# Low halves of the first layer's weight tiles: written by VectorE instead of GpSimd

## The chip, the cores and the metric

The kernel runs on one core of one Trainium2 chip. The metric is device time in microseconds (us) from launch to end. Before the change three runs gave a median of 1679.97 us (1676.94 to 1680.24).

## What is computed

```python
def _attn_ref(q, k, v):                       # 8 batches, 8 heads, 576 rows, 64 columns
    q_s = softmax(q, axis=-1); k_s = softmax(k, axis=2)
    kv = np.einsum('bhsd,bhse->bhde', k_s, v)
    return np.einsum('bhsd,bhde->bhse', q_s, kv)

def reference(q, k, v, moe_w_in, moe_w_out, moe2_w_in, moe2_w_out):
    x = attn.transpose(0, 2, 1, 3).reshape(4608, 512)
    h = x @ moe_w_in;  x = (h * sigmoid(1.702 * h)) @ moe_w_out       # 512 -> 2048 -> 512
    h = x @ moe2_w_in; return np.maximum(0.01 * h, h) @ moe2_w_out
```

All is float32. The two softmaxes are written out in the reference with max, exp and sum.

## The kernel before

**Split numbers.** A matrix product is made of three passes: each float32 operand is split into a high half (rounded by a ScalarE cast, line 80, `split_hi`) and a low half (the operand less the high half, line 83, `split_lo`). TensorE then adds high x high, low x high and high x low. Every weight tile and every activation tile therefore needs a cast on ScalarE and one subtraction before TensorE can finish its product. In the trace all subtractions have line 83 and are told apart by their tile.

**Chunks and layers.** The 4608 tokens are nine chunks of 512. In a layer, after some start, chunks go in pairs. The first product of a pair is a 2x2 block scheme that saves multiplications: `quad_step` (eight per pair, n = 0 to 7) takes a quarter of `w_in` (four tiles wa, wb, wc, wd, line 621), with sums and differences of token blocks (x and xb from xr) as the other operand. The second product (`g2`, line 668) goes over 16 slices f of `w_out` (tile wo) and accumulates in four PSUM banks (acc). `pair_first` runs the eight quad steps of a pair with the second product of its first chunk two slices behind; `pair_second` then runs the second product of the other chunk, f = 0 to 15.

**Where the low halves in question are made.** Chunk 1 of layer 0 goes through `pair_second` with `made` true: for f = 2 to 15 the float32 slice of `w_out` is loaded from DRAM (o, line 276, two buffers, and line 857 to 860: the load of slice f + 3 stands ahead of the making of slice f + 2), cast by ScalarE (`make_wo`), subtracted (`make_wo_low`, line 283) and stored to DRAM for the later pairs (line 284). The store and the load share SyncE's queue, which is in order. The quad tiles for chunk pair (2, 3) of layer 0 are made too: `s0` loads a quarter of `w_in` (w, line 215), `s1` makes two sums and differences from it (t, lines 222 to 224), and `make_tile` with `make_low` (line 241) split the four tiles and store them (line 242): wa (m = 0) and wd (m = 3) are plain quarters of w, wb and wc come from t. That is eight quads; quad 0 is made during `pair_second` of chunk 1, quad n + 1 during quad step n. All later pairs of the layer load split tiles from DRAM. In layer 1 the same is made again from its own weights.

**What stands around it.** In the same stretch the attention of chunks 2 and 3 runs in pieces between the products: row maxima of k (kmx, kma, km, kmb, lines 379 to 406), k less its maximum (line 412), exp, the product with v (kvp, line 427), its scale (krs and kv, lines 439 to 444), q (qmx, qt, qsm, qs, lines 450 to 469), its transpose (qtp, line 481), and the product that gives the tokens (pxt, line 503). After the start these use a single PSUM bank, `att` in `bank`, for kma, kmb, qtp and kvp. Then `build_pair` makes the token blocks (lines 549 and 566) and splits them (x, xb). Activations g of the second product have their own low halves (gl).

**What sets the order.** Each engine works through its own queue in order. The program is written with gaps into which work is put, and a scheduler of the framework then orders the instructions of all engines by its own estimate of when each is ready. Changing the engine of an instruction therefore also moves others.

Of the kernel before, what the change touches and what calls it, by code (L numbers as in the profile page):

```python
# [8 lines left out]
F32 = mybir.dt.float32  # L9
F32R = mybir.dt.float32r  # L10
AF = mybir.ActivationFunctionType
ALU = mybir.AluOpType
# [14 lines left out]
def tile_softmax_linear_attention_two_mlps(  # L27
# [16 lines left out]
    nc = tc.nc  # L44
# [34 lines left out]
    def split_hi(src, hi):  # L79
        nc.scalar.copy(hi, src)  # L80

    def split_lo(src, hi, lo, engine=nc.vector):
        engine.tensor_tensor(out=lo, in0=src, in1=hi.bitcast(F32), op=ALU.subtract)  # L83

# [41 lines left out]
    WO = {}  # L128
# [38 lines left out]
    def c4(f):  # L167
        w = cvt.pop(f)[:, 1, :].bitcast(F32)
        split_lo(w[:, 0:T].rearrange("p (b n) -> p b n", b=2), WI[f][:, :, 0, :], WI[f][:, :, 1, :])
        split_lo(w[:, T : 2 * T], WO[f][:, 0, :], WO[f][:, 1, :])  # L170
        n, i = divmod(f, 2)
        for b in range(2):
            nc.sync.dma_start(out=w4d[0][n][:, BLOCK[i, b], :], in_=w[:, 2 * P * b : 2 * P * (b + 1)])
        if f < 2:
            nc.sync.dma_start(out=wod[0][f], in_=WO[f].rearrange("p h n -> p (h n)").bitcast(F32))
        else:
            nc.sync.dma_start(out=o32d[0][f], in_=w[:, T : 2 * T])
# [60 lines left out]

    def make_low(i, n, m):
        src, to = halves.pop(m)  # L240
        split_lo(src, to[:, :, 0, :], to[:, :, 1, :], nc.gpsimd if i == 0 and m in (0, 3) else nc.vector)
        nc.sync.dma_start(
            out=wqd[i][n][:, 2 * m * T : (2 * m + 2) * T], in_=to.rearrange("p b h n -> p (b h n)").bitcast(F32)
        )
# [23 lines left out]
    o32 = {}  # L268
# [11 lines left out]
        split_hi(o32[f], WO[f][:, 0, :])  # L280

    def make_wo_low(i, f):
        split_lo(o32.pop(f), WO[f][:, 0, :], WO[f][:, 1, :], nc.vector if i else nc.gpsimd)
        nc.sync.dma_start(out=wod[i][f], in_=WO[f].rearrange("p h n -> p (h n)").bitcast(F32))


# [563 lines left out]
    def pair_second(layer, c, per_step):  # L850

        acc = new_acc()

        made = (layer, c) == (0, 1)
        ready(1)
        if made:
            load_o32(0, 2)
        for f in range(NF):
            if made and f + 3 < NF:
                load_o32(0, f + 3)  # L860
            if f + 2 < NF:
                if made:
                    make_wo(f + 2)
                    make_wo_low(0, f + 2)
                else:
                    load_wo(layer, f + 2)
                ready(f + 2)
            run(per_step.get(f, ()))
            if f < NF - LAG:
                g2(layer, f, acc, range(KT))  # L870
        return (layer, c, acc)
# [148 lines left out]
    def first_quad(layer, c):  # L1020

        if not sums_of(layer, c):
            return [lambda m=m: load_quad(layer, 0, m) for m in (0, 1, 2, 3)]
        made = (0, 3, 1, 2)
        pieces = [lambda: s0(layer, 0), lambda: s1(layer, 0)]
        for m in made:
            pieces += [lambda m=m: make_tile(layer, 0, m), lambda m=m: make_low(layer, 0, m)]
        pieces += [lambda: s0(layer, 1), lambda: s1(layer, 1)]
        return pieces

    def work_of(layer, c, nxt):
        def work(n, gaps):
            m = n + 1
            if m < NQ:
                if sums_of(layer, c):
                    def make(at, j):
                        gaps[at].append(lambda: make_tile(layer, m, j))
                        gaps[at + 1].append(lambda: make_low(layer, m, j))

                    make(1, 0)  # L1040
                    make(4, 3)
                    if m + 1 < NQ:
                        gaps[5].append(lambda: s0(layer, m + 1))
                    make(6, 1)
                    make(8, 2)
                    if m + 1 < NQ:
                        gaps[9].append(lambda: s1(layer, m + 1))
                else:
                    gaps[1].append(lambda: load_quad(layer, m, 1))
                    gaps[4].append(lambda: load_quad(layer, m, 0))  # L1050
                    gaps[5].append(lambda: load_quad(layer, m, 2))
                    gaps[9].append(lambda: load_quad(layer, m, 3))
            if (layer, c) == (1, 0):
                gaps[3].append(lambda: make_wo(2 * n))
                gaps[4].append(lambda: make_wo_low(1, 2 * n))
                gaps[7].append(lambda: make_wo(2 * n + 1))
                gaps[8].append(lambda: make_wo_low(1, 2 * n + 1))
                if n + 1 < NQ:
                    gaps[9].append(lambda: load_o32(1, 2 * n + 2))
                    gaps[9].append(lambda: load_o32(1, 2 * n + 3))  # L1060
            else:
                gaps[2].append(lambda: load_wo(layer, 2 * n))
                gaps[7].append(lambda: load_wo(layer, 2 * n + 1))
# [123 lines left out]
```

## Time and profile before

| | |
|---|---|
| median of three runs | 1679.97 us (1676.94 to 1680.24) |
| the profiled execution: its own time, its span | 1681.45 us, 1679.7 us |
| TensorE matmul (PE) busy | 1624.8 us, 97% of the span, 7552 instructions |
| VectorE (DVE) busy | 1050.3 us, 63%, 1649 instructions |
| ScalarE (ACT) busy | 640.5 us, 38%, 1088 instructions |
| GpSimd (POOL) busy | 120.8 us, 7%, 236 instructions |
| mean granted TensorE clock | 0.992 of full speed |

The profile was taken on one execution; its span runs from the first to the last instruction. PE is matmul, PEld weight load. An idle time in brackets behind an instruction names what its engine waited for. Full granted clock (1.00) is 2.4 GHz, half is 1.2 GHz.

### The profile page before, as it was taken

What the parts mean: (1) busy time and instruction counts of PE and PEld (TensorE: products, weight loads), DVE (VectorE), ACT (ScalarE), POOL (GpSimd) and SP (SyncE); (2) the same over time, 40 slices, a digit from 0 to 9 for tenths busy, and PEclk for the clock granted to TensorE, in tenths of its full rate; (3) what the DMA queues carried; (4) which work ended last, traced back from release to release, by engine and by line L of the source; (5) the groups of instructions that cost most, each with busy time, mean ns of one, the idle gap of its engine ahead of it and who ended that gap; (6) DMA issues with size and microseconds to landing.
All of it is one profiled execution on the core that took longest, in us unless ns stands there. A gap on an engine that the chain in (4) does not pass through costs nothing.

```text
span 1679.7 us, 21410 instructions
## 1 busy us (share of the span) xinstructions
PE 1624.8 (97%) x7552; PEld 1300.8 (77%) x7552; DVE 1050.3 (63%) x1649; ACT 640.5 (38%) x1088; POOL 120.8 (7%) x236
## 2 busy tenths in 40 slices
PE   5799998999999999999999999999999999999999
PEld 3577776777777778777888888888888888888887
DVE  8999657887767767667434877355734473445222
ACT  5667554555444445345223434211321132112222
POOL 1110243231100000000000000000000000000000
PEclk9999998999999999999999999999999999999999
DMA  7666476878888887878786876766676666667662
GB/s 216 216 217 204 124 236 238 291 259 265 271 272 253 248 265 238 287 255 305 261 270 219 312 279 230 253 219 187 208 252 209 196 216 216 213 190 225 200 208 100
DMA packets 192875, 391.50 MB, mean 233 GB/s; under 512 B 57600, under 2 KB 99584, under 8 KB 192768
## 3 DMA queue, kind: packets, MB, share of 16 engines
q1 hardware_dynamic: 192768, 390.14, 71.2%
q8 instruction: 60, 0.98, 0.2%
q14 instruction: 47, 0.39, 0.1%
HBM read 304.61 MB, written 85.46 MB: 232 GB/s over the span
## 4 chain that ended last, share of the span: by engine, by line
PE 80%; DMA 6%; DVE 4%; issue 2%; ACT 2%; POOL 2%; SPq 1%; ACTq 0%; POOLq 0%; DVEq 0%
PE acc L668 40%; PE hb L621 11%; PE h L608 9%; PE ha L621 8%; PE hc L621 8%; DMA o<-cv 2%; DMA w<-cv 2%; PE pxt L503 1%; DMA w<-w 1%; PE kvp L427 1%; DVE cv L125 1%; POOL wo L83 1%; DVE cv L121 1%; DVE gl L83 1%; POOL qt L451 0%
## 5 line engine op out<-in xcount | busy, mean ns | idle before, releaser
L668 PE MATMUL acc<-gh,wo 128*128 128x512 f32 x1152 | 367.5, 401 | 9.2 <-ACT gh L80 4.2
L668 PE MATMUL acc<-wo,gh 128*128 128x512 f32 x1152 | 355.8, 390 | 0.0
L668 PEld LDWEIGHTS acc<-gh,wo 128*128 128x128 f32 x1152 | 214.6, 191 | 57.4 <-ACT gh L80 5.5
L668 PEld LDWEIGHTS acc<-wo,gh 128*128 128x128 f32 x1152 | 216.2, 188 | 46.7 <-issue 0.4
L668 PE MATMUL acc<-gl,wo 128*128 128x512 f32 x576 | 226.5, 396 | 0.0
L668 PE MATMUL acc<-wo,gl 128*128 128x512 f32 x576 | 225.2, 391 | 0.0
L608 PE MATMUL h<-x,wi 128*128 128x512 f32 x768 | 194.5, 402 | 5.3 <-ACT wi L80 5.3
L608 PEld LDWEIGHTS h<-x,wi 128*128 128x128 f32 x768 | 143.2, 189 | 44.1 <-ACT wi L80 7.7
L83 DVE TENSOR_TENSOR gl<-gb,gh 128x512 fp32r<-128x512 f32 x128 | 91.0, 715 | 121.7 <-ACT gh L80 121.5
L621 PE MATMUL ha<-x,wa 128*128 128x512 f32 x624 | 165.6, 400 | 0.0
L80 ACT CAST gh<-gf 128x512 fp32r<-128x512 f32 x160 | 99.0, 619 | 136.9 <-PE acc L668 63.9
L83 DVE TENSOR_TENSOR gl<-gf,gh 128x512 fp32r<-128x512 f32 x160 | 110.4, 690 | 58.8 <-ACT gh L80 57.5
L80 ACT CAST gh<-gb 128x512 fp32r<-128x512 f32 x128 | 79.2, 621 | 161.3 <-PE acc L668 160.7
L621 PEld LDWEIGHTS ha<-x,wa 128*128 128x128 f32 x624 | 116.5, 188 | 29.0 <-issue 1.9
L668 PEld LDWEIGHTS acc<-gl,wo 128*128 128x128 f32 x576 | 109.3, 190 | 24.9 <-DVE gl L83 0.4
L668 PEld LDWEIGHTS acc<-wo,gl 128*128 128x128 f32 x576 | 108.1, 188 | 23.6
L777 DVE TENSOR_TENSOR u<-hb,p 128x512 f32<-128x512 f32 x56 | 38.5, 688 | 118.8 <-PE hb L621 110.0
L621 PE MATMUL hb<-x,wc 128*128 128x512 f32 x384 | 100.3, 396 | 0.8 <-DVE v L777 0.8
L621 PE MATMUL hb<-xb,wb 128*128 128x512 f32 x336 | 87.9, 396 | 2.7 <-ACT xb L80 2.7
L621 PEld LDWEIGHTS hb<-x,wc 128*128 128x128 f32 x384 | 71.7, 187 | 18.8 <-DVE v L777 1.9
L621 PEld LDWEIGHTS hb<-xb,wb 128*128 128x128 f32 x336 | 63.3, 189 | 18.2 <-ACT xb L80 3.0
L621 PE MATMUL hc<-x,wb 128*128 128x512 f32 x288 | 76.0, 399 | 0.9 <-DVE p L777 0.9
(131 smaller groups left out, 2073.7 us busy)
## 6 DMA issues: line engine op xcount, KB each, us to landing
wo<-wo SPq DMA_DIRECT2D x274, 512.0 KB, 4.2
wa<-wq SPq DMA_DIRECT2D x40, 512.0 KB, 4.0
wb<-wq SPq DMA_DIRECT2D x40, 512.0 KB, 4.6
wc<-wq SPq DMA_DIRECT2D x40, 512.0 KB, 4.7
raw<-in_moe_w_in_dram SPq DMA_DIRECT2D x32, 512.0 KB, 4.3
raw<-in_moe_w_out_dram SPq DMA_DIRECT2D x32, 512.0 KB, 4.9
wi<-wq SPq DMA_DIRECT2D x32, 512.0 KB, 4.5
wd<-wq SPq DMA_DIRECT2D x40, 256.0 KB, 3.2
```

The costliest lines, as they stand in the source:

```text
L80: nc.scalar.copy(hi, src)
L83: engine.tensor_tensor(out=lo, in0=src, in1=hi.bitcast(F32), op=ALU.subtract)
L121: nc.vector.scalar_tensor_tensor(out=w[:, o], in0=hw, scalar=0xC0000000, in1=w[:, o], op0=ALU.bitwise_and, op1=ALU.bitwise_or)
L125: nc.vector.tensor_tensor(out=w, in0=w, in1=low, op=ALU.add)
L427: nc.tensor.matmul(pk[h * D : (h + 1) * D, 0 : D + 1], rest[0][:, h, :] if r == R and rest else km[:, h, r, :], vm[:, h, r, :] if r < R el ...
L503: nc.tensor.matmul(pv[:, :, a:e], kvb[b, j], t[:, :, a:e], start=True, stop=True)
L608: nc.tensor.matmul(h, WI[f][:, b, wh, o * P : (o + 1) * P], xs[f"a{side}{b + 1}"][xh][:, o, :], start=(i == 0), stop=(i == n - 1),)
L621: nc.tensor.matmul(h, w[:, wh, o * P : (o + 1) * P], xo[xh][:, o, :], start=(start and i == 0), stop=(i == 5), skip_group_check=not start,)
L668: nc.tensor.matmul(acc[d], lhsT, rhs, start=(f == 0 and i == 0), stop=(f == NF - 1 and i == 2))
L777: add = lambda out, h, t: nc.vector.tensor_tensor(out=out, in0=h, in1=t, op=ALU.add)
```

## The change

The optional engine of `split_lo` goes away, and the three places that called it take VectorE always. In layer 0 the low halves of wo for f = 2 to 15 (14 instructions) and of wa and wd in the eight quads (16 instructions) were on GpSimd; they are now on VectorE. Layer 1 had them on VectorE already. Nothing else is edited.

```diff
-    def split_lo(src, hi, lo, engine=nc.vector):
-        engine.tensor_tensor(out=lo, in0=src, in1=hi.bitcast(F32), op=ALU.subtract)
+    def split_lo(src, hi, lo):
+        nc.vector.tensor_tensor(out=lo, in0=src, in1=hi.bitcast(F32), op=ALU.subtract)
...
     def make_low(i, n, m):
         src, to = halves.pop(m)
-        split_lo(src, to[:, :, 0, :], to[:, :, 1, :], nc.gpsimd if i == 0 and m in (0, 3) else nc.vector)
+        split_lo(src, to[:, :, 0, :], to[:, :, 1, :])
...
     def make_wo_low(i, f):
-        split_lo(o32.pop(f), WO[f][:, 0, :], WO[f][:, 1, :], nc.vector if i else nc.gpsimd)
+        split_lo(o32.pop(f), WO[f][:, 0, :], WO[f][:, 1, :])
```

The scheduler's order moves with it. First place, VectorE's queue at the start of `pair_second` of chunk 1 (o_2267 and o_2269 are the float32 slices f = 2 and 3; w_2371 and t_2439 are quad 0's quarter and its sums):

```order
 L401 TENSOR_REDUCE km<-kma 128x1
-L83 TENSOR_TENSOR gl<-gb,gh 128x512
+L83 TENSOR_TENSOR wo<-o_2267,wo 128x512
+L83 TENSOR_TENSOR gl<-gb,gh 128x512
+L83 TENSOR_TENSOR wo<-o_2269,wo 128x512
 L222 TENSOR_TENSOR t_2439<-w_2371 128x2x256
+L83 TENSOR_TENSOR wa<-w_2371,wa 128x2x256
+L412 TENSOR_TENSOR kt<-kt,kmb 128x640
+L83 TENSOR_TENSOR gl<-gb,gh 128x512
 L223 TENSOR_TENSOR t_2439<-w_2371,t_2439 128x256
-L412 TENSOR_TENSOR kt<-kt,kmb 128x640
```

Between km and line 412 there were a gl and lines 222 and 223; now there are two low halves of wo, a gl, line 222 and a low half of wa.

Second place, VectorE's queue of the changed kernel near the end of the same `pair_second`, where the token blocks of chunks 2 and 3 are built (o_2603 and o_2627 are slices f = 12 and 13):

```order
L566 TENSOR_TENSOR xr<-xr 128x1024
L379 TENSOR_REDUCE kmx<-kt 128x128
L83 TENSOR_TENSOR gl<-gb,gh 128x512
L83 TENSOR_TENSOR x<-xr,x 128x1024 x2
L549 TENSOR_TENSOR xr<-xr 128x1024
L83 TENSOR_TENSOR wo<-o_2603,wo 128x512
L83 TENSOR_TENSOR gl<-gb,gh 128x512
L83 TENSOR_TENSOR xb<-xr,xb 128x1024
L83 TENSOR_TENSOR wo<-o_2627,wo 128x512
```

The low half of slice 12 now stands behind the sum of line 566, two low halves of x and a difference of line 549; before it was in GpSimd's queue, where nothing of these stood.

Third place, TensorE's queue where the first quad step meets the last slices (acc_2259 to acc_2262 are the four banks of the second product):

```order
 L621 MATMUL ha<-x,wa 128x512 x6
 L396 MATMUL kma<-ident,kmx 128x128
-L621 MATMUL hb<-xb,wb 128x512 x3
 L668 MATMUL acc_2259<-gh,wo 128x512
 L668 MATMUL acc_2260<-gh,wo 128x512
+L668 MATMUL acc_2261<-gh,wo 128x512
+L668 MATMUL acc_2262<-gh,wo 128x512
 L668 MATMUL acc_2259<-gh,wo 128x512
 L668 MATMUL acc_2259<-gl,wo 128x512
```

Half of the product hb, which needs xb, stood ahead of slice 12; now it comes behind slices 12 and 13.

## Rows read from the trace of the kernel before

**Rows 1.** Busy time of stretches (length, then PE, PEld, DVE, ACT, POOL, clock).

```profile
218.00:296.00 78.00, 68.60 (x308) 52.98 (x306) 55.37 (x70) 38.58 (x65) 32.65 (x30) 0.91 0.73 249
...
260.00:280.00 20.00, 15.78 (x51) 11.80 (x51) 12.19 (x15) 6.94 (x11) 8.04 (x5) 0.74 0.53 198
296.00:400.00 104.00, 103.73 (x562) 82.77 (x563) 86.14 (x146) 55.04 (x100) 28.27 (x47) 1.00 0.81 269
880.00:1030.00 150.00, 150.00 (x652) 122.05 (x651) 102.59 (x166) 58.62 (x97) 0.00 (x0) 1.00 0.76 265
```

**Rows 2.** TensorE's waits, 210 to 400 us: total us, times, longest us.

```profile
PE hb L621 <- ACT xb L80: 2.7, 1, 2.7
PE acc L668 <- POOL wo L83: 2.3, 2, 1.6
PE pxt L503 <- ACT kv L444: 2.1, 2, 1.8
PE qtp L481 <- DVE kt L412: 1.5, 1, 1.5
PE hb L621 <- DVE u L777: 1.1, 1, 1.1
```

**Rows 3.** GpSimd's groups by form (busy us, mean ns, idle before).

```profile
L83 POOL TENSOR_TENSOR wo<-o,wo 128x512 fp32r<-128x512 f32 x14 | 22.1, 1593 | 30.0 <-ACT wo L80 27.8 <-DMA kt<-in_k_dram 2.2
...
L83 POOL TENSOR_TENSOR wa<-w,wa 128x512 fp32r<-128x512 f32 x8 | 11.8, 1477 | 23.3 <-ACT wa L80 16.5 <-PE kvp L427 6.8
L83 POOL TENSOR_TENSOR wd<-w,wd 128x512 fp32r<-128x512 f32 x8 | 10.8, 1350 | 18.9 <-ACT wd L80 18.9
```

**Rows 4.** Line 83 by form: durations ns min, median, max; first and last start us.

```profile
L83 DVE TENSOR_TENSOR wo<-o,wo x16: 682/692/693, 914.6 to 1026.6; 128x512 fp32r<-128x512 f32 x16
```

**Rows 5.** VectorE's groups by form, 216 to 297 us.

```profile
L83 DVE TENSOR_TENSOR gl<-gb,gh 128x512 fp32r<-128x512 f32 x13 | 12.3, 950 | 2.8 <-ACT gh L80 2.7
...
L223 DVE TENSOR_TENSOR t<-w,t 128x256 f32<-128x256 f32 x3 | 3.7, 1234 | 0.1
...
L222 DVE TENSOR_TENSOR t<-w 128x512 f32<-128x512 f32 x3 | 3.2, 1054 | 0.7 <-DMA w<-w 0.7
```

**Rows 6.** VectorE's timeline, 219 to 232 us (start us, length us, instruction).

```profile
219.56 1.61 DVE L83 TENSOR_TENSOR gl<-gb,gh 128x512 fp32r<-128x512 f32 x1
221.09 1.78 DVE L222 TENSOR_TENSOR t<-w 128x512 f32<-128x512 f32 x1
222.91 1.38 DVE L223 TENSOR_TENSOR t<-w,t 128x256 f32<-128x256 f32 x1
224.22 0.81 DVE L412 TENSOR_TENSOR kt<-kt,kmb 128x640 f32<-128x640 f32 x1
...
231.62 0.14 DVE L439 TENSOR_SCALAR krs<-kvp 128x1 f32<-128x1 f32 x1
```

**Rows 7.** GpSimd's timeline, three of its low halves of wo.

```profile
219.33 3.00 POOL L83 TENSOR_TENSOR wo<-o,wo 128x512 fp32r<-128x512 f32 x2
...
252.36 3.50 POOL L83 TENSOR_TENSOR wo<-o,wo 128x512 fp32r<-128x512 f32 x2 [2.20 <-DMA kt<-in_k_dram]
264.47 4.70 POOL L83 TENSOR_TENSOR wo<-o,wo 128x512 fp32r<-128x512 f32 x2 [8.61 <-ACT wo L80]
```

**Rows 8.** SyncE's queue, 205 to 300 us: its longest wait.

```profile
SPq L284 <- POOL wo L83: 33.6, 9, 8.2
```

**Rows 9.** Loads of the float32 slices o.

```profile
DMA to landing us min/median/max: 3.2/3.9/5.0
```

**Rows 10.** VectorE's timeline in two of the later quad steps.

```profile
328.84 0.69 DVE L777 TENSOR_TENSOR u<-hb,p 128x512 f32<-128x512 f32 x1 [0.42 <-PE kma L396]
...
360.51 0.41 DVE L223 TENSOR_TENSOR t<-w,t 128x256 f32<-128x256 f32 x1
...
364.81 0.69 DVE L777 TENSOR_TENSOR u<-hb,p 128x512 f32<-128x512 f32 x1 [2.22 <-PE kma L396]
365.42 0.28 DVE L401 TENSOR_REDUCE km<-kma 128x1 f32<-128x128 f32 x1
```

## The prediction

> **What bounds the kernel now.** I read the summary of the page first: PE is busy for 97% of the span, so only stretches where it is not are worth anything. Then I asked where GpSimd makes low halves (its groups by form, [rows 3]): 14 of wo and 16 of wa and wd, 44.7 us together, all between 219 and 386 us. The busy time by stretches [rows 1] splits that in two. From 218 to 296 us, the second product of chunk 1 with the start of the first quad steps, PE is busy for 68.60 of 78.00 us and its clock is 0.91 of full. From 296 to 400 us, the later quad steps, PE is busy for 103.73 of 104.00 us at full clock. So the first stretch alone can gain, and the second can only lose.
>
> What the first stretch loses: 78.00 - 68.60 = 9.4 us of idle time [rows 1]. A mean clock of 0.91 over 78 us is (1 - 0.91) x 2 x 78 = 14.0 us at the half level, of which (1 - 0.74) x 2 x 20 = 10.4 lie between 260 and 280 us [rows 1]. About 1.6 us of this is idle already (the longest wait for a GpSimd wo [rows 2]), and the rest does in 12.4 us what 6.2 would do, so 6.2 us are lost. Together 15.6 us: that is all there is to win.
>
> TensorE's waits [rows 2] name the ends: 2.7 us for an xb cast, 2.3 for wo from GpSimd, 2.1 for kv from ScalarE, 1.5 for line 412 and 1.1 for u, both on VectorE. Only 2.3 us name GpSimd. The next question is what made VectorE late.
>
> **What GpSimd did to VectorE.** The timelines of both [rows 6, 7] lie side by side: while GpSimd runs two low halves of wo from 219.33 to 222.33, VectorE's gl takes 1.61 us and its line 222 takes 1.78; their undisturbed length is about 0.69 [rows 4, 10]. Line 223 takes 1.38 there and 0.41 where GpSimd is quiet [rows 6, 10]. Both sides suffer: a pair of GpSimd's takes 3.00, 3.50 or 4.70 us [rows 7]. Over 216 to 297 us the groups give the excess [rows 5]: gl 13 x (0.95 - 0.69) = 3.4 us, line 223 3 x (1.23 - 0.41) = 2.5, line 222 3 x (1.05 - 0.69) = 1.1, so 7.0 us from these three groups alone.
>
> **The change part by part.** Removed from GpSimd: 30 instructions, 44.7 us [rows 3]. It is busy for 7% of the span, so this is worth only what waited for it. Added to VectorE: 30 instructions of a kind that it does in 0.69 us [rows 4]; followed by another of its own, one costs 0.61 from start to start (364.81 to 365.42 [rows 10]). That is 18.3 us, of which 20 x 0.61 = 12.2 fall before 296 us (14 wo and three pairs wa, wd), against at least 7.0 given back there. VectorE is busy for 55.37 of 78 us [rows 1], so it would have 60.6 at most to do; in the 66 us that I expect of this stretch, that is dense but fits.
>
> The Trainium skill (Perfetto Trace Analysis, Optimizing Scalar/DVE Operations) advises that work may be offloaded from a saturated VectorE, even to GpSimd, and adds that it might not help, because the two share a read port. By the first half alone this change would cost up to those 18.3 us; by the second half much of it was being paid already, and the stretched rows side with the second half here.
>
> Now by places, in the order of time. At the head (first place of the change), line 412 stood behind a stretched gl and lines 222 and 223, and started at 224.22 [rows 6]. Now five instructions stand between 219.56 and it, 5 x 0.61 = 3.05, so it starts near 222.6, 1.6 us earlier: the wait of 1.5 us on it [rows 2] goes. Next is kv, whose scale krs started at 231.62 [rows 6]. In the new queue 11 instructions stand between line 412 and krs, nine full ones and lines 223 and 224: 222.6 + 0.8 + 9 x 0.61 + 2 x 0.41 = 229.7, 1.9 us earlier. TensorE comes 1.5 us earlier but has one matmul more to do ahead of pxt (0.23, the 150 us over 652 of [rows 1]), so of its longest wait for kv, 1.8 us, about 1.2 remain.
>
> The slices wo come by a loop: a low half frees a buffer, SyncE (in order) stores it and loads the slice after next, the load lands 3.9 us later [rows 9], ScalarE casts it, then comes the next low half. SyncE waited 33.6 us for GpSimd's wo here [rows 8]. Two low halves take 1.2 us instead of 3.0 to 4.7 [rows 7], so each turn of the loop, two slices, is some 2 to 3 us shorter, and the 2.3 us of waits for wo should go. TensorE wants 12 x 0.23 = 2.8 us for a slice.
>
> What is late next is slice 12 (second place). Its low half now stands behind line 566, a reduction, a gl, two low halves of x and line 549. Counted in instructions of 512 elements, that is 2 + 2 + 1 + 4 + 2 = 11, and its own, 12 x 0.61 = 7.3 us. The gl of slice 13 is among them, and those of slices 11 and 12 stand just ahead, so I take VectorE to reach line 566 when TensorE begins slice 11. TensorE has slice 11, the product ha and four passes for the high half of slice 12, (12 + 6 + 4) x 0.23 = 5.1 us. So it waits about 2.2 us there. The wait of 2.7 us for xb goes, as that product now comes behind slices 12 and 13 (third place) and xb is made while they run.
>
> The wait of 1.1 us for u comes from line 223 ahead of it on VectorE; u now stands ahead of lines 222 and 223, so it goes. In the first quad step w's second quarter is loaded behind one store fewer, so I cost this at nothing; if it landed late, line 222 would hold up the v behind it.
>
> The later quad steps: two low halves more for each, 1.2 us of a step of (364.81 - 328.84) / 2 = 18.0 us [rows 10]. VectorE is busy for 83% (86.14 of 104 [rows 1]), hence 14.9 us of a step, and 16.1 after. The new wa stands ahead of u, which waits 0.42 us for TensorE in one step and 2.22 in another [rows 10]; line 223, stretched by the same wa before, gives back what it takes. I cost it at nothing; without that cover it is 0.2 to 1.2 us a step.
>
> **The sum.** Lost before 15.6; after, 1.2 + 2.2 = 3.4 idle. I keep one half-level spell as before's shorter one, 14.0 - 10.4 = 3.6 us, which costs 1.8, since the trace has it behind waits of 1.5 and 1.8 and I leave one of 2.2. Gain 15.6 - 3.4 - 1.8 = 10.4 us. The profiled execution took 1681.45, so 1671.0; it lay 1.5 above the median of the runs, so I forecast 1670 us. Bounds from both sides: everything gone gives 1680 - 15.6 = 1664; nothing gone gives 1680.
>
> **The rivals.** First, the same direction but less: VectorE holds slices 12 to 15 up while it builds the blocks, TensorE waits as long as before there, and the long half-level spell of 10.4 us comes back. Then only the head (1.5 + 0.6 + 1.8 of clock) and u (1.1) are won, 5.0 us: 1675. For it: the pile of 7.3 us ahead of slice 12. Against it: it needs VectorE 2 us later than counted.
>
> Second, no change: the loads bind the loop, not the halves. A load is 3.2 to 5.0 us [rows 9], and with SyncE's other transfers between, TensorE could meet the same slices late by as much. Then the waits only change their names and 0 to 3 us are won: 1678. Against it: SyncE's longest wait is for GpSimd [rows 8].
>
> Third, slower: VectorE becomes the bound of the quad steps. In eight steps 2 x 0.61 each go straight onto TensorE's path, because u, v and p free the banks that the next products need: 9.8 us, and with nothing won at the head 1690. It decides once VectorE's 3 us of slack in a step are less than its waits for the others. For it: u has only 0.42 us to spare in one step. Against it: in layer 1 the same tiles are made wholly on VectorE from 880 to 1030 us, and PE is busy for 150.00 of 150 us [rows 1], though without attention work beside it.
>
> **How the numbers follow.** The forecast (gain 7 to 15.6) has 0.60, the first rival 0.17, the second 0.14, the third 0.09. Runs of this kernel can tell 0.2% (3.4 us) from no change: faster is 0.77, within it 0.14, slower 0.09. The range goes from 1664.5, all waits gone, up to 1678, which leaves the third rival and half of the second outside; the likeliest case's own range is 1664.5 to 1673.
>
> **What would show it.** In the changed profile: PE idle from 218 on down from 9.4 to some 3.5 us, with slice 12 the longest wait and no wait for line 412 or u; VectorE's gl and lines 222 and 223 near 0.69 and 0.41; the clock between 260 and 280 us near full; later quad steps still of 18.0 us. Wrong it would be if the quad steps grew longer, if the half level stayed for 10 us, or if the waits for wo were now for loads.

## The result, and the profile after

The changed kernel takes 1665.66 us (median of 4 runs, 1661.06 to 1666.67), the kernel before 1679.49 (4 runs beside it, 1676.94 to 1680.24). The ratio is 0.9915, 95% interval 0.9893 to 0.9937. That is faster by 13.8 us; 10 were forecast.

The busy time by stretches comes first (length, then PE, PEld, DVE, ACT, POOL, clock; changed kernel). It answers to [rows 1].

```profile
218.00:296.00 78.00, 76.45 (x386) 60.23 (x385) 68.59 (x111) 45.75 (x79) 3.83 (x15) 1.00 0.89 306
260.00:280.00 20.00, 19.90 (x85) 15.45 (x84) 19.74 (x30) 12.10 (x20) 2.12 (x2) 1.00 0.92 312
```

In the 78 us where everything was to be won, TensorE is now idle for 78.00 - 76.45 = 1.55 us instead of 9.4, and its clock is full instead of 0.91. It runs 386 matmuls there instead of 308. From 260 to 280 us VectorE is busy for 19.74 of 20 us: that stretch has hardly any slack on VectorE left, and TensorE is still busy for 19.90.

TensorE's waits from 210 to 400 us (total us, times, longest us) are only these two, where [rows 2] has five:

```profile
PE pxt L503 <- ACT kv L444: 1.2, 2, 1.0
PE acc L668 <- DVE wo L83: 0.4, 1, 0.4
```

VectorE's timeline in the changed kernel (start us, length us, instruction) answers to [rows 6] in its first five lines and to [rows 10] in its last two; the two between belong to slice 12. The stage began 0.93 us later here than before, for a reason ahead of it (the first matmul of acc in it starts at 215.70 and started at 214.77), so 0.93 is to be taken off when starts are compared.

```profile
220.77 0.68 DVE L83 TENSOR_TENSOR gl<-gb,gh 128x512 fp32r<-128x512 f32 x1
...
222.15 0.69 DVE L222 TENSOR_TENSOR t<-w 128x512 f32<-128x512 f32 x1
...
223.41 0.81 DVE L412 TENSOR_TENSOR kt<-kt,kmb 128x640 f32<-128x640 f32 x1
...
224.74 0.42 DVE L223 TENSOR_TENSOR t<-w,t 128x256 f32<-128x256 f32 x1
...
230.23 0.15 DVE L439 TENSOR_SCALAR krs<-kvp 128x1 f32<-128x1 f32 x1
...
251.07 1.22 DVE L566 TENSOR_TENSOR xr<-xr 128x1024 f32<-128x1024 f32 x1
...
257.55 0.69 DVE L83 TENSOR_TENSOR wo<-o,wo 128x512 fp32r<-128x512 f32 x1
...
316.33 0.69 DVE L777 TENSOR_TENSOR u<-hb,p 128x512 f32<-128x512 f32 x1 [0.53 <-PE kma L396]
...
334.04 0.69 DVE L777 TENSOR_TENSOR u<-hb,p 128x512 f32<-128x512 f32 x1 [1.06 <-PE kma L396]
```

The stretched instructions are short again: gl 0.68 us for 1.61, line 222 0.69 for 1.78, line 223 0.42 for 1.38. So VectorE does more in less time. The last two lines are one quad step apart: 334.04 - 316.33 = 17.7 us; before, two took 36.0 [rows 10].

VectorE's groups by line, 216 to 297 us (busy us, mean ns, idle before), answer to [rows 5]:

```profile
L83 DVE TENSOR_TENSOR wo<-o,wo 128x512 fp32r<-128x512 f32 x14 | 9.6, 686 | 3.0 <-ACT wo L80 3.0
L83 DVE TENSOR_TENSOR gl<-gb,gh 128x512 fp32r<-128x512 f32 x13 | 8.9, 687 | 2.0 <-ACT gh L80 1.9
```

The 14 low halves that took GpSimd 22.1 us [rows 3] take VectorE 9.6, and 3.4 of these come back from gl alone (12.3 to 8.9).

TensorE's timeline around slice 12, the place at which the prediction saw the longest wait left:

```profile
252.55 0.61 PE L668 MATMUL acc<-gh,wo 128*128 128x512 f32 x2
...
255.28 1.57 PE L621 MATMUL ha<-x,wa 128*128 128x512 f32 x6
...
258.29 0.50 PE L668 MATMUL acc<-gh,wo 128*128 128x512 f32 x1 [0.41 <-DVE wo L83]
```

Slice 11 begins at 252.55, and the pass that needs slice 12's low half comes after 5.3 us and waits 0.41. The low half itself is the instruction that VectorE began at 257.55, above. SyncE's queue, 205 to 290 us, its longest wait (answers to [rows 8]):

```profile
SPq L284 <- DVE wo L83: 23.9, 11, 3.7
```

The longest time that SyncE stands at a low half is 3.7 us instead of 8.2.

### The profile page after: what moved, and what is told of

Same layout as the page of the kernel before. It is cut to its first block, busy times and chain, and to the rows that moved or that the text cites. A ratio compares the mean times of both kernels' runs of the same rounds, so it can differ in the third digit from the quotient of the medians.

```text
span 1664.6 us, 21423 instructions
## 1 busy us (share of the span) xinstructions
PE 1618.2 (97%) x7552; PEld 1296.0 (78%) x7552; DVE 1052.7 (63%) x1679; ACT 639.8 (38%) x1088; POOL 74.1 (4%) x206
## 4 chain that ended last, share of the span: by engine, by line
PE 79%; DMA 7%; DVE 5%; ACT 2%; issue 2%; SPq 1%; POOL 1%; ACTq 0%; DVEq 0%; POOLq 0%
PE acc L668 40%; PE hb L621 11%; PE h L608 10%; PE ha L621 8%; PE hc L621 8%; DMA w<-cv 2%; DMA o<-cv 2%; PE pxt L503 1%; DVE gl L83 1%; DMA w<-w 1%; DMA raw<-in_moe_w_out_dram 1%; PE kvp L427 1%; ACT cv L107 1%; DMA o<-o 1%; DMA wo<-wo 1%
## 5 line engine op out<-in xcount | busy, mean ns | idle before, releaser
L668 PE MATMUL acc<-gh,wo 128*128 128x512 f32 x1152 | 363.5, 397 | 6.7 <-ACT gh L80 4.3
L83 DVE TENSOR_TENSOR gl<-gb,gh 128x512 fp32r<-128x512 f32 x128 | 87.6, 688 | 119.7 <-ACT gh L80 114.9
L782 ACT COPY p<-ha 128x512 f32<-128x512 f32 x56 | 32.8, 586 | 112.0 <-PE ha L621 112.0
```

Source lines behind the costliest of these rows:

```text
L83: nc.vector.tensor_tensor(out=lo, in0=src, in1=hi.bitcast(F32), op=ALU.subtract)
L668: nc.tensor.matmul(acc[d], lhsT, rhs, start=(f == 0 and i == 0), stop=(f == NF - 1 and i == 2))
L782: nc.scalar.copy(p1, a)
```

## The experiments

Each run was timed beside the kernel before, and its ratio is to that one: 1680.94 us beside the first four runs, 1679.33 beside the next four, 1680.06 beside the last four. Layers are counted from 0, as above; the recorded expectations call layer 1 "layer 2". Theory A: GpSimd's subtractions hold VectorE up while both read SBUF, and that costs time where TensorE stands behind VectorE, in the w_out product of chunk 1. Rival B: only the slow step on GpSimd counts, in the loop of low half, store, load and cast. Rival C: only the new order of the work counts.

**Only the wo low halves moved.** In the kernel before:

```
-        split_lo(o32.pop(f), WO[f][:, 0, :], WO[f][:, 1, :], nc.vector if i else nc.gpsimd)
+        split_lo(o32.pop(f), WO[f][:, 0, :], WO[f][:, 1, :], nc.vector)
```

> Only the 14 low halves of wo go to VectorE; wa and wd stay on GpSimd. Theory (the gain lies before 296 us, where the wo are made): nearly all of it, 1667 to 1669 us; what is missing is the wait for u behind a stretched line 223, about 1 us, and any stretch by the three pairs wa, wd there. Rival (the 16 wa and wd are as much to blame, since they stretch VectorE in all eight quad steps): about half of the 14 us, 1672 us.

Measured: 1667.35 us (1662.25 to 1669.98), ratio 0.9916 (0.99 to 0.9932). The stretch, in the columns of the first fence:

```profile
218.00:296.00 78.00, 75.89 (x382) 59.40 (x381) 68.47 (x102) 45.68 (x78) 13.48 (x22) 1.00 0.87 301
```

The 14 wo instructions carry the whole gain. The 16 of wa and wd stay on GpSimd, and the time shows no cost of them.

**Only the wa and wd low halves moved.**

```
-        split_lo(src, to[:, :, 0, :], to[:, :, 1, :], nc.gpsimd if i == 0 and m in (0, 3) else nc.vector)
+        split_lo(src, to[:, :, 0, :], to[:, :, 1, :], nc.vector)
```

> Only the 16 low halves of wa and wd go to VectorE; the wo stay on GpSimd. Theory: the wait for u goes (1.1 us) and little else, 1677 to 1679 us, TensorE still idle for some 8 us from 218 to 296 and at the half level for about 10 us. Rival (both parts count alike): 1672 us. Rival (VectorE is the bound of the quad steps, so that these 16 cost 0.6 us each): 1685 us or more.

Measured: 1680.55 us (1675.47 to 1684.39), ratio 0.9992 (0.9981 to 1.0003): no change. By stretches:

```profile
218.00:296.00 78.00, 69.79 (x314) 54.25 (x314) 56.15 (x78) 38.87 (x66) 25.77 (x25) 0.91 0.74 256
260.00:280.00 20.00, 15.76 (x52) 11.78 (x51) 12.06 (x16) 6.92 (x10) 8.02 (x5) 0.74 0.51 192
```

Here line 223 is short again (0.415 us; stretched by wa before) and TensorE's wait of 1.1 us for u is gone, but its longest wait for kv grew from 1.8 to 2.4 us, and the 1 to 3 us that the theory gave can't be told from nothing. The clock from 260 to 280 us stayed at 0.74. In the quad steps either engine can make these halves.

**GpSimd kept busy beside.** The changed kernel, with a subtraction of 480 columns on GpSimd beside every moved low half. It reads the high half that was just cast and writes a tile of its own that nobody reads. On TensorE, VectorE and ScalarE the order is that of the changed kernel.

```
+    def beside(*his):
...
+            nc.gpsimd.tensor_tensor(out=d, in0=d, in1=hi[:, 0:n].bitcast(F32), op=ALU.subtract)
...
         split_lo(o32.pop(f), WO[f][:, 0, :], WO[f][:, 1, :])
+        if i == 0:
+            beside(WO[f][:, 0, :])
```

> As the changed kernel, with the same order on TensorE, VectorE and ScalarE, but behind each of the 30 low halves GpSimd makes a subtraction of nearly the same size (480 of 512 columns, the high half from a scratch tile into that scratch tile) that nobody waits for. Theory A (GpSimd hurt by holding VectorE up): gl, lines 222 and 223 are stretched again, and much of the gain goes, 1670 to 1675 us. Theory B (GpSimd hurt as a slow step on the path, in the loop of load, cast, low half, store): nothing changes, 1665 to 1667 us. Rival C (the new order alone brought the gain): nothing changes either, 1665 to 1667 us.

Measured: 1675.42 us (1672.12 to 1677.59), ratio 0.9966 (0.9954 to 0.9978): 9.8 us slower than the changed kernel by the medians, 8.6 by the two ratios. TensorE never waits for what was added. VectorE does once, for 1.6 us, ahead of the line 394 below, where the changed kernel waits 1.3 for a load; SyncE does once, for 1.8 us. The stretch; TensorE's three largest waits from 210 to 400 us; VectorE's groups from 216 to 297 us (most lines stand 15 further down in this kernel):

```profile
218.00:296.00 78.00, 67.39 (x320) 50.87 (x319) 71.50 (x91) 38.83 (x65) 42.10 (x35) 1.00 0.76 258
260.00:280.00 20.00, 14.49 (x58) 9.77 (x57) 20.00 (x20) 8.92 (x14) 10.87 (x5) 1.00 0.57 204
```

```profile
PE acc L683 <- DVE wo L83: 5.5, 5, 1.6
PE pxt L518 <- ACT kv L459: 2.7, 3, 1.1
PE qtp L496 <- DVE kt L427: 1.4, 1, 1.4
```

```profile
L83 DVE TENSOR_TENSOR wo<-o,wo 128x512 fp32r<-128x512 f32 x14 | 14.5, 1037 | 4.0 <-ACT wo L80 4.0
L83 DVE TENSOR_TENSOR gl<-gb,gh 128x512 fp32r<-128x512 f32 x13 | 10.6, 812 | 1.2 <-ACT gh L80 1.2
L83 DVE TENSOR_TENSOR xb<-xr,xb 128x1024 fp32r<-128x1024 f32 x3 | 6.5, 2187 | 0.0
...
L394 DVE TENSOR_REDUCE kmx<-kt 128x128 f32<-128x640 f32 x3 | 3.9, 1314 | 1.8 <-POOL idle L132 1.6 <-DMA kt<-in_k_dram 0.2
```

The same instructions in the same order are longer: wo 1037 ns for 686, gl 812 for 687, xb 2187 for 1387. From 260 to 280 us VectorE is busy without a break and gets through 20 instructions instead of 30. TensorE is idle for 10.6 us instead of 1.55, and these 9.1 us account for the loss; more than half of its waits, 5.5 us, are for low halves of wo that VectorE makes. The wait for line 412 is back, and the waits for kv have grown from 1.2 to 2.7 us. So contention is shown to cost by itself, and B and C, which put this run at 1665 to 1667, fall as the whole of it.

Three things this run does not show. It does not size the contention of the kernel before: GpSimd is busy for 42.10 us of the stretch here, for 32.65 there [rows 1]. It does not bring back all that was expected: the means of lines 222 and 223 stay at 675 and 488 ns, and the clock stays full. And it leaves room for B and C as parts: TensorE waited 2.3 us for GpSimd's own wo [rows 2], and the wait of 2.7 us for xb stays away here, where the order is the new one. How the 13.8 us divide among the three stays open.

The Trainium skill (SBUF — State Buffer, Who interferes with whom) says that a VectorE instruction with two inputs in SBUF contends with a GpSimd instruction that reads SBUF, and that a reduction doesn't. The rows of wo, gl and xb agree with the first. For the second, two lines of the kernel before lie beside the GpSimd pair of 264.47 to 269.17 us [rows 7]:

```profile
264.45 1.22 DVE L83 TENSOR_TENSOR xb<-xr,xb 128x1024 fp32r<-128x1024 f32 x1
...
266.92 0.68 DVE L461 TENSOR_REDUCE qsm<-qt 128x8 f32<-128x512 f32 x1
```

Line 461, a reduction, takes 0.68 us there, as it does at 218.25 us, where GpSimd makes no subtraction: that agrees. But xb, with two inputs, isn't stretched there either; GpSimd's pair took 4.70 us, the longest of [rows 7]. Which of the two engines is held up in a given pair these runs don't settle.

**Three buffers for the loads of o.** The kernel before, with o and p1 in three buffers instead of two, each load one slice earlier, and one buffer for qmx instead of two (to make room).

```
-            else pool["cv"].tile([P, T], F32, tag="p1", name="o32", bufs=2)
+            else pool["cv"].tile([P, T], F32, tag="p1", name="o32", bufs=3)
...
-        mx = sb.tile([P, 2, R], F32, tag="qmx", name="qmx", bufs=2)
+        mx = sb.tile([P, 2, R], F32, tag="qmx", name="qmx", bufs=1)
...
-            if made and f + 3 < NF:
-                load_o32(0, f + 3)
+            if made and f + 4 < NF:
+                load_o32(0, f + 4)
```

> As the kernel before, low halves on GpSimd, but three buffers for the float32 slices o instead of two and each load one slice earlier (qmx has one buffer instead of two, for room). Theory B (the loop through the buffers sets the pace, GpSimd's length being one part of it): waits for wo and the long half-level spell go, 1670 to 1674 us. Theory A (GpSimd holds VectorE up, whatever the buffers): line 412, kv and xb stay late, 1677 to 1680 us.

Measured: 1665.03 us (1659.95 to 1666.74), ratio 0.9898 (0.9883 to 0.9914). As fast as the changed kernel, which looked like the loop of rival B. But the stretches say otherwise:

```profile
218.00:296.00 78.00, 69.61 (x324) 55.13 (x323) 59.97 (x75) 40.86 (x70) 32.10 (x29) 0.93 0.77 271
...
1150.00:1300.00 150.00, 150.00 (x663) 124.23 (x662) 77.84 (x110) 36.07 (x55) 0.00 (x0) 1.00 0.69 220
```

The stretch that the loop should mend is hardly better than before (69.61 against 68.60, clock 0.93), and TensorE's longest wait for a GpSimd wo there is 3.6 us instead of 1.6. Most of the gain lies in layer 1, where nothing waits: 663 matmuls in 150 us at full clock, and 654 in the kernel before and the changed one. By that rate the 800 us from 880 us on are 11 us shorter, an estimate from the two counts. This run doesn't support B; a new question is open.

**Which part of it: four kernels.** One buffer for qmx in the kernel before, and nothing else:

> The kernel before with one buffer instead of two for qmx; the low halves stay on GpSimd. It asks what gave the 15 us of the run with three buffers, whose layer 2 ran 663 matmuls per 150 us of TensorE instead of 654. Theory that the third buffer gave it (and the earlier loads of o): 1680 us here, 654 matmuls in 150 us of layer 2. Rival that the qmx buffer gave it, by the order of the work or by where the tiles lie: about 1667 us and 663 matmuls in 150 us.

The buffers without the earlier loads:

> The kernel before with three buffers for p1 and o32 and one for qmx, the loads of o issued where they were. Theory that it is the number of buffers, through where the tiles lie: 1667 us, 663 matmuls in 150 us of layer 2, and in the first layer's w_out quads the same waits for GpSimd's low halves as before. Rival that the earlier loads gave it: 1680 us and 654 matmuls.

All of it in the changed kernel, and one buffer for qmx alone in the changed kernel:

> The changed kernel with three buffers for p1 and o32, the loads of o one slice earlier, and one buffer for qmx. Theory that the gain of the change (14 us, by waits and half clock at the first layer's w_out quads) and that of the three buffers (15 us, of which 11 in layer 2 by matmuls that follow each other at 0.2262 us instead of 0.2294) are separate: 1653 us, and 663 matmuls in 150 us of layer 2. Rival that both are one and the same, a matter of order: 1665 us.

> The changed kernel with one buffer instead of two for qmx. Theory that the third buffer matters and not qmx: 1666 us, as the changed kernel, 654 matmuls in 150 us of layer 2. Rival that qmx alone sets the faster matmuls: 1654 us and 663 matmuls.

Measured: one qmx buffer in the kernel before 1664.74 us (1658.87 to 1672.64), ratio 0.9917 (0.9897 to 0.9937), 664 matmuls in 150 us; with three buffers for o and p1 1662.26 (1658.04 to 1666.15), ratio 0.9901 (0.9885 to 0.9918), 664; all of it in the changed kernel 1652.63 (1647.55 to 1657.53), ratio 0.9844 (0.9826 to 0.9863); one qmx buffer in the changed kernel 1648.99 (1646.05 to 1651.13), ratio 0.982 (0.9807 to 0.9832). The theory of the third buffer falls: one buffer of 32 bytes per partition less does it all, and the third buffers and the earlier loads add nothing beside it that can be told from the scatter. Its gain adds to that of the change (1664.74 to 1648.99 is 15.8 us), and the last kernel beats both of this case.

**Place or order: three kernels.** One buffer less should move every tile placed behind it by 32 bytes, and it also changes the order of the work. (No trace shows addresses; the places are taken from the program.) To tell these apart, an unused tile of 32 bytes is put ahead of all others, which leaves the order on TensorE, VectorE and ScalarE as it was:

```
+    pad = sb.tile([P, 8], F32, tag="pad", name="pad")
+    nc.gpsimd.memset(pad, 0.0)
     ident = sb.tile([P, P], F32, tag="ident", name="ident")
```

In the changed kernel:

> The changed kernel with one more tile of 32 bytes per partition ahead of all others in SBUF, filled once by GpSimd and never read; on TensorE, VectorE and ScalarE every instruction stands where it stood. Theory that the 15 us of the single qmx buffer come from where the tiles lie (one buffer of qmx is 32 bytes, so all behind it moved by as much): 1650 us, 663 or 664 matmuls in 150 us of layer 2, and the matmuls with wa, wb and wc at 389 ns instead of 395. Rival that they come from the order of the work, which one buffer less also changed: 1666 us, 654 matmuls, 395 ns.

In the changed kernel with one qmx buffer:

> The changed kernel with one buffer for qmx, and the same unused tile of 32 bytes in SBUF, so that the tiles lie where they lay in the changed kernel while the order on TensorE, VectorE and ScalarE is that of the single buffer. Theory of the place: 1665 us, 654 matmuls in 150 us of layer 2, 395 ns. Rival, the order: 1649 us, 664 matmuls, 389 ns.

In the kernel before:

> The kernel before with the same unused tile of 32 bytes, its order otherwise kept; the low halves on GpSimd. Theory that place and the change are separate: 1664 us with 664 matmuls in 150 us of layer 2, so that the change is worth 14 us at this place of the tiles too, against the changed kernel with the tile. Rival that the change and the place work on the same matmuls: less than 8 us between the two.

Measured: 1657.42 us (1656.61 to 1660.07), ratio 0.987 (0.9848 to 0.9891); 1662.14 (1660.78 to 1669.5), ratio 0.9906 (0.9884 to 0.9929); and 1673.2 (1669.87 to 1681.27), ratio 0.9965 (0.9949 to 0.9981). TensorE's groups by form from 1150 to 1300 us, those of ha, show it best (count, busy us, mean ns): the changed kernel; with one qmx buffer; with the unused tile; with both.

```profile
L621 PE MATMUL ha<-x,wa 128*128 128x512 f32 x84 | 21.9, 395 | 0.0
```

```profile
L621 PE MATMUL ha<-x,wa 128*128 128x512 f32 x87 | 22.1, 389 | 0.0
```

```profile
L623 PE MATMUL ha<-x,wa 128*128 128x512 f32 x84 | 21.5, 391 | 0.0
```

```profile
L623 PE MATMUL ha<-x,wa 128*128 128x512 f32 x84 | 22.1, 395 | 0.0
```

And the last kernel's stretch, which has 664 matmuls without the unused tile:

```profile
1150.00:1300.00 150.00, 150.00 (x654) 122.41 (x653) 77.07 (x108) 36.05 (x55) 0.00 (x0) 1.00 0.67 219
```

The order of the single qmx buffer with the tiles behind it back at their place gives 654 matmuls and 395 ns, as the changed kernel; and the order kept with the tiles moved gives 658 and 391. So the place of the tiles sets the rate, not the order. The gain of the change itself is not a matter of place: the kernel before, the changed one and the one with GpSimd busy beside all have 654. My number for the unused tile (664 matmuls, 1650 and 1664 us) was wrong: 32 bytes more ahead of all tiles are worth some 7 us, half as much as 32 bytes fewer at qmx. Which tile's address counts, and how, stays open.

With the same place on both sides the change is worth 1673.2 - 1657.42 = 15.8 us, so it and the place are separate, as expected.

**The rest of GpSimd's reading moved too.** The changed kernel with one qmx buffer, and q's subtraction on VectorE:

```
-        (nc.vector if c == 0 else nc.gpsimd).tensor_tensor(
+        nc.vector.tensor_tensor(
```

> The changed kernel with one buffer for qmx, and the subtraction of the maximum from q (32 instructions of 1385 ns on GpSimd, 44.3 us) on VectorE too; GpSimd then reads no large tile. Theory that contention with GpSimd costs wherever both read: TensorE's 2.3 us wait for qt goes and VectorE's work beside q gets shorter, 1644 us. Rival that it costs only where TensorE's next step waits for VectorE or GpSimd, as in the w_out quads, and that 32 more instructions of about 0.69 us on VectorE (22 us) take the gain back: 1649 us or more.

Measured: 1650.15 us (1649.02 to 1653.91), ratio 0.9829 (0.9807 to 0.9851), against 1648.99 without the edit. The rival was right: VectorE is busy for 1067.65 us instead of 1053.39 in all, TensorE's one wait of 2.3 us for qt goes, its waits for ScalarE's wi grow from 0.7 to 3.9 us, and nothing is won.

## Why the prediction was right, step by step

**Where and how much.** That the gain would come from 218 to 296 us, and be 15.6 us at most there, held. What remains there is 1.2 + 0.4 = 1.6 us of waits at full clock, so 15.6 - 1.6 = 14.0 by the prediction's own sum. The median fell by 13.8. The end of the stretch is seen at u of the same quad step, before and after:

```profile
311.10 0.69 DVE L777 TENSOR_TENSOR u<-hb,p 128x512 f32<-128x512 f32 x1 [2.73 <-DMA qt<-in_q_dram]
```

```profile
298.16 0.69 DVE L777 TENSOR_TENSOR u<-hb,p 128x512 f32<-128x512 f32 x1 [1.88 <-DMA qt<-in_q_dram]
```

It starts 12.9 us earlier, and 13.9 counted from the first acc of the stage. The two profiled executions lie 14.8 us apart, so the 0.93 us lost ahead of the stage come back behind it: from 500 to 800 us TensorE's wait for a load of wo is 1.9 us instead of 2.6, and the mean clock from 640 to 880 us is 1.00 instead of 0.99. The prediction had nothing of this, and whether the change did it is not shown.

**A premise that didn't hold.** The prediction began with "only stretches where it is not are worth anything", that is, where TensorE is not busy. That did no harm to the forecast, but the single qmx buffer gained 15 us, most of them where TensorE is busy for 150 of 150 us at full clock.

**The cause.** That VectorE was late because GpSimd's subtractions stretched its own was argued from three groups of rows. The kernel with GpSimd busy beside shows that such stretching can cost 8.6 to 9.8 us; that it cost as much in the kernel before stays an inference from those rows.

**The head.** Line 412 was to start near 222.6 and started at 223.41 - 0.93 = 222.5; krs near 229.7, and it was 229.3. The wait of 1.5 us for line 412 is gone, and of the longest for kv 1.0 us remain (1.2 predicted). The waits for xb and u are gone as well, as predicted.

**Slice 12, the term that was mis-sized.** The prediction let VectorE reach line 566 when TensorE begins slice 11, and so had a wait of 2.2 us. It reached it at 251.07, 1.5 us ahead of 252.55, and the wait was 0.41. The pile itself was right: 257.55 - 251.07 = 6.5 us to the low half's start, where 11 x 0.61 = 6.7 had been counted, and TensorE took 5.3 us for what was counted as 5.1. When the two engines meet there was assumed, not derived from rows, and the assumption was 1.5 us too late for VectorE.

**The half-level spell, the other mis-sized term.** The prediction kept one, at a cost of 1.8 us, behind that wait. The clock is 1.00 in the stretch. The two terms together are 1.8 + 1.8 = 3.6 us, the difference between 10.4 and 14.0.

**Later quad steps.** Costed at nothing, and rightly: 17.7 us for the step shown, and moving wa and wd alone gave a ratio of 0.9992. VectorE as the bound of these steps, the slower rival, didn't come.

**The rivals.** VectorE did not hold slices 12 to 15 up beyond 0.41 us, and TensorE has no wait for a load of o. Its one wait for wo is for a low half.

## What to carry to other kernels

Before handing VectorE's work to GpSimd, look at what runs on VectorE at those times: a subtraction on GpSimd stretched its neighbours on VectorE from 0.69 to as much as 1.78 us, and of 9.7 us of TensorE's waits only 2.3 named GpSimd. Here the offload cost time where TensorE's next step stood behind these engines: 14 instructions cost some 14 us, 16 others nothing that could be told. And when a control edit gives a gain, look in which stretch it lies before crediting it to the reason it was made for: here some 15 us came from 32 bytes.

## What was not expected of the hardware

The place of tiles in SBUF, moved by 32 bytes, changed the rate of back-to-back matmuls at the full clock in layer 1: 654, 658 or 664 in 150 us, which is 0.2294 to 0.2259 us for each, 1.5%.

With GpSimd busy beside, TensorE was idle for 10.6 us in waits of at most 1.6 us, and its granted clock stayed at 1.00. The kernel before was idle for 9.4 us, with a wait of 2.7, and had 0.91. The fall of the clock therefore did not follow from the idle time of the stretch alone.
